# Sums of Strassen products in the GLU units: from VectorE additions to TensorE accumulation seeded by ScalarE

## The chip, the core and the metric

The kernel runs as one launch on one NeuronCore of a Trainium2 chip. Its time is the device time of the launch in microseconds (us), taken as the median of several runs. The engines named here are TensorE (PE in the profile; PEld is its weight load), VectorE (DVE), ScalarE (ACT), GpSimd (POOL) and SyncE (SP), which issues most DMAs. Each engine works through its own instructions in order; between engines there are only semaphores. TensorE writes its products into PSUM, eight banks of 128 x 512 fp32 each.

## The reference

With S = 2048 rows, D = 512 columns and F = 1792 hidden columns:

```python
xn = layernorm(x)
a, b = xn @ Wd_re.T, xn @ Wd_im.T          # 512 x 512
y  = Ws_re @ a - Ws_im @ b                 # 2048 x 2048
h  = gelu(xn @ w_gate) * (xn @ w_up)       # 512 x 1792, tanh form
out = x + y + h @ w_down                   # 1792 x 512
```

## The kernel before

The kernel has three stages. The first makes the layer norm and the sequence transform (names `z`, `m`, `pan`), the second the hidden transform (`y`). The third, from about 399 us to the end, computes the gated part, and the change lies there. All matrix products are done in three passes: each operand is split into a high part (a rounded copy, made by ScalarE, `split_hi`, L68) and a low part (the difference, made by VectorE, `split_lo`, L73), and `mm3` (L81) issues high x high, high x low and low x high.

The third stage runs 28 units, `unit(n)` (L552). A unit computes a block of 256 hidden columns x 1024 rows of gate (n even) or up (n odd) as one step of Strassen's scheme in Winograd's form: seven half-size products instead of eight, each a group of six matmuls over 512 columns (`product`, L462), and their sums. The products are numbered 0 to 6 by the operands they take (`xT0` to `xT6` in the trace). The four blocks of the result are, with p0 to p6 for the products: block (0,0) = p0 + p1; a sum p0 + p5 on which block (0,1) builds by adding p4 and p2 in turn; a sum p0 + p5 + p6 to which p4 is added for block (1,1); and p0 + p5 + p6 + p3 for block (1,0). In the kernel before, p0 stands in bank `a` and is copied by ScalarE to an SBUF tile `p1` (L589); p5, p6 and p3 accumulate one after another in bank `b`, p4 and then p2 in bank `c`; VectorE adds `p1` to bank `b` three times (L590 into `q6`, L600 into `w`, L610 into `p1`), and bank `c` twice (L601 into `w`, L616 into `q6`).

Between the products stand fills: `fill()` (L577) takes from a list the next piece of other TensorE work of the same length, six matmuls of the down projection (`dn`) or, in the first units, of the hidden transform (`y`). `FILL` (L519) gives units 0 and 1 two fills, units 2 to 5 three and all others four. A unit asks for a fill after its third product, after product 1, and twice after product 2; where fewer are allowed the last ones fall out, so that behind product 2 of units 0 and 1 the next unit's product 0 follows at once, and behind that of units 2 to 5 after one fill.

The finished blocks go through `first` and `second`. In even units `first` is `gate` (L468): ScalarE takes the GELU of the block into `s`. In odd units it is `up_1` (L472): VectorE multiplies the block into `s`, ScalarE makes the high part `hh`; `second` is `up_2`, VectorE's low part `hl`. The second halves of the last two blocks are carried into the next unit. `run(share)` places background work between these steps: the splits of the next unit's weights (`wh`, `w` on ScalarE, `wl`, `w` on VectorE; two conversions are begun ahead), of the down weights (`wdh`, `wdl`, in even units and unit 1), sums of weights (`ws`, L424) and, in units 7 to 13, splits of the second half of the rows (`xT`). The order of each engine's instructions is that in which the code issues them; nothing reorders them.

Of the kernel before, what the change touches and what calls it, by code (L numbers as in the profile page):

```python
# [11 lines left out]
AF = mybir.ActivationFunctionType  # L12
# [22 lines left out]
def fnet_geglu_kernel(ctx: ExitStack, tc: tile.TileContext, x, xt, cs, dh, wgu, wd, out):  # L35
# [7 lines left out]
    nc = tc.nc  # L43
# [8 lines left out]
    def slot(name, dtype=F32, shape=(P, D)):  # L52
        return mem.tile(list(shape), dtype, name=name, tag="mem")

    def ps_tile(name):
        return psum.tile([P, D], F32, name=name, tag="ps")
# [24 lines left out]
    def mm3(ps, a, sl, b, first, last, resumed=False, part=slice(3)):  # L81

        for r, (u, v) in list(enumerate(((0, 0), (0, 1), (1, 0))))[part]:
            nc.tensor.matmul(ps, a[u][:, sl], b[v], start=first and r == 0, stop=last and r == 2,  # L84
                             skip_group_check=resumed)

    def cols(j):
        return slice(j * P, (j + 1) * P)
# [206 lines left out]
    def flush():  # L295
        while pend:
            split_lo(*pend.pop(0))
# [63 lines left out]
    def load_xT(sp, t):  # L361
        for d in range(ND):
            load_xr(sp, t, d, xnt[sp, t, d])
# [47 lines left out]
    def load_w(n):  # L411
        if n < 2 * NP:
            wx[n] = [slot("wx", F32, (P, 2, HD)) for _ in range(2)]
            for i in range(2):
                nc.sync.dma_start(wx[n][i].rearrange("p a b -> p (a b)"), wgu[n % NP, i])
# [31 lines left out]
    def split_w(n):  # L447
        for k in range(4):
            split(*weight_split(n, k))

    def load_wd(n):

        for i in range(2 if n < 2 * NP else 0):
            wdl[n // 2, i] = slot("wd")
            nc.sync.dma_start(wdl[n // 2, i], wd[n % NP // 2, i])
# [6 lines left out]
    def product(n, k, ps, first=False):  # L462
        for i in range(2):
            mm3(ps, wl[n, k], cols(i), xT[n // NP, k, i], first and i == 0, i == 1, resumed=not first)
# [17 lines left out]
    def load_acc(n):  # L482
        acc[n] = slot(f"acc{n}")
        nc.sync.dma_start(acc[n], parked[n])
# [25 lines left out]
    carry = []  # L510

    def more_items(q):

        i = q % (NP // 2)
        if i % 2 == 0:
            qs = [q - 1, q] if i else [q]
            items.extend([lambda j=j, p=p: down(qs, j, p) for j in range(SPT) for p in qs])
# [3 lines left out]
    def background(n):  # L521

        work = []

        def splits(f, *args, cost=2):
            t = []

            def begin():
                t.append(f(*args))
                split_hi(*t[0])  # L530
            work.append((begin, lambda: split_lo(*t[0]), cost))

        if 0 < n < 2 * NP - 1:
            for k in range(4):
                splits(weight_split, n + 1, k, cost=2 if k < 3 else 1)
        if n == 1 or n % 2 == 0 and n:
            for i in range(2):
                splits(down_split, n, i)
        if n + 2 < 2 * NP:
            for f in weight_sums(n + 2):  # L540
                work.append((None, f, 1))
        if -7 <= n - NP < 0:
            for i in range(2):
                splits(xT_split, 1, (0, 1, 2, 4, 5, 6, 3)[n - NP + 7], i)
        u = n - NP + 10
        if u in (3, 4):
            work.append((None, lambda: sums_xT(1, u - 3), 6))
        if u == 7:
            work.append((None, lambda: t4_xT(1), 4))
        return work  # L550

    def unit(n):  # L552
        left = FILL.get(n, 4)
        load_w(n + 2)
        if n - NP + 10 in (0, 2):
            load_xT(1, (n - NP + 10) // 2)
        work = background(n)
        total, done, begun = sum(w[2] for w in work), 0, 0

        def run(share):  # L560

            nonlocal done, begun
            upto = share * total
            while work and done + work[0][2] / 2 <= upto:
                begin, end, cost = work.pop(0)
                if begun:
                    begun -= 1
                elif begin:
                    begin()
                end()  # L570
                done += cost
            while begun < min(2, len(work)):
                if work[begun][0]:
                    work[begun][0]()
                begun += 1

        def fill():  # L577
            nonlocal left
            left -= 1
            return items.pop(0)() if items and left >= 0 else lambda: None  # L580

        first, second = (gate, lambda *a: None) if n % 2 == 0 else (up_1, up_2)
        if n % 2 == 0 and n:
            more_items(n // 2 - 1)
        a, b, c = ps_tile("a"), ps_tile("b"), ps_tile("c")
        product(n, 0, a, True)
        product(n, 5, b, True)
        p1, q6, w = slot("p1"), slot("q6"), slot("w")
        nc.scalar.activation(p1, a, AF.Copy)  # L589
        nc.vector.tensor_add(q6, b, p1)  # L590
        while carry:
            carry.pop(0)()
        flush()
        product(n, 4, c, True)
        d0 = fill()
        run(.2)
        d0()
        product(n, 6, b)
        run(.35)
        nc.vector.tensor_add(w, b, p1)  # L600
        nc.vector.tensor_add(w, c, w)  # L601
        product(n, 1, a)
        d1 = fill()
        first(n, (0, 0), a)
        first(n, (1, 1), w)
        second(n, (0, 0), a)
        d1()
        run(.55)
        product(n, 3, b)
        nc.vector.tensor_add(p1, b, p1)  # L610
        second(n, (1, 1), w)
        if n == 0:
            split_w(1)
        run(.75)
        product(n, 2, c)
        nc.vector.tensor_add(q6, c, q6)  # L616
        if n % 2 == 1:
            load_wd(n + 1)
        if n % NP == 1:
            for j in range(SPT):  # L620
                load_acc(n // NP * SPT + j)
        first(n, (1, 0), p1)
        first(n, (0, 1), q6)
        d2, d3 = fill(), fill()
        d2()
        run(1)
        carry.extend([lambda: second(n, (1, 0), p1), lambda: second(n, (0, 1), q6), d3])

    def turn_step(k):

# [143 lines left out]
    for n in range(2 * NP):  # L774
        unit(n)
# [36 lines left out]
```

## Time and profile before

| | |
|---|---|
| time, median of 3 runs | 835.08 us (835.06 to 836.07) |
| time of the profiled execution | 835.21 us |
| its span, first to last instruction | 833.4 us |
| TensorE busy | 828.0 us (99%), 3638 matmuls |
| VectorE busy | 679.6 us (82%) |
| ScalarE busy | 364.8 us (44%) |
| granted TensorE clock, mean | 0.999 of 2.4 GHz |

Busy shares are averages over the three stages. Matmuls overlap: one takes 0.39 us, the next starts 0.227 us after it. The start of a matmul, not its end, tells whether TensorE waited. On ScalarE and VectorE, too, a next instruction may start some 0.1 us before the recorded end of the one ahead.

### The profile page before, as it was taken

What the parts mean: (1) busy time and instruction counts of PE and PEld (TensorE: products, weight loads), DVE (VectorE), ACT (ScalarE), POOL (GpSimd) and SP (SyncE); (2) the same over time, 40 slices, a digit from 0 to 9 for tenths busy, and PEclk for the clock granted to TensorE, in tenths of its full rate; (3) what the DMA queues carried; (4) which work ended last, traced back from release to release, by engine and by line L of the source; (5) the groups of instructions that cost most, each with busy time, mean ns of one, the idle gap of its engine ahead of it and who ended that gap; (6) DMA issues with size and microseconds to landing.
All of it is one profiled execution on the core that took longest, in us unless ns stands there. A gap on an engine that the chain in (4) does not pass through costs nothing.

```text
span 833.4 us, 10707 instructions
## 1 busy us (share of the span) xinstructions
PE 828.0 (99%) x3638; PEld 681.6 (82%) x3638; DVE 679.6 (82%) x1227; ACT 364.8 (44%) x672; POOL 9.5 (1%) x22
## 2 busy tenths in 40 slices
PE   9999999999999999999999999999999999999998
PEld 6888888888888888888888888888888888888886
DVE  6677998979799988999688879889877887776852
ACT  6787544633354335554343344434434334333410
POOL 0000000000100010000000000000000000000000
PEclk9999999999999999999999999999999999999999
DMA  9900448563896929852505310101216322120002
GB/s 335 358 14 1 164 161 282 173 219 115 284 334 224 293 107 324 244 169 67 205 23 177 101 52 30 72 26 51 76 51 215 112 56 73 34 68 25 2 9 93
DMA packets 60711, 112.92 MB, mean 135 GB/s; under 512 B 6864, under 2 KB 6896, under 8 KB 60656
## 3 DMA queue, kind: packets, MB, share of 16 engines
q1 hardware_dynamic: 59376, 108.05, 38.6%
q0 software_dynamic: 1280, 4.20, 1.3%
q8 instruction: 28, 0.46, 0.2%
q14 instruction: 27, 0.22, 0.1%
HBM read 99.61 MB, written 12.60 MB: 135 GB/s over the span
## 4 chain that ended last, share of the span: by engine, by line
PE 94%; DVE 3%; DMA 1%; issue 0%; ACT 0%; DVEq 0%; ACTq 0%
PE m L84 24%; PE dn L84 18%; PE b L84 14%; PE z L84 10%; PE c L84 9%; PE a L84 9%; PE y L84 9%; DVE psl L73 1%; DMA xr<-in_xt 1%; PE warm L658 1%; DVE m L314 1%; DMA wd<-in_wd 0%; DMA pan<-in_cs 0%; DVE ws L424 0%; DVE pan L267 0%
## 5 line engine op out<-in xcount | busy, mean ns | idle before, releaser
L68 ACT ACTIVATE psh<-pan 128x512 fp32r<-128x512 f32 x168 | 97.6, 627 | 106.4 <-DVE pan L267 32.5
L73 DVE TENSOR_TENSOR psl<-pan,psh 128x512 fp32r<-128x512 f32 x168 | 105.3, 684 | 3.8 <-ACT psh L68 3.6
L68 ACT ACTIVATE hh<-s 128x512 fp32r<-128x512 f32 x56 | 34.4, 633 | 125.9 <-DVE s L475 120.8
L84 PE MATMUL dn<-wdh,hh 128*128 128x512 f32 x224 | 87.1, 389 | 0.0
L84 PE MATMUL dn<-wdl,hh 128*128 128x512 f32 x224 | 87.1, 389 | 0.0
L84 PE MATMUL dn<-wdh,hl 128*128 128x512 f32 x224 | 87.1, 389 | 0.0
L84 PE MATMUL m<-psh,xch 128*128 128x512 f32 x192 | 74.8, 389 | 0.0
L84 PE MATMUL m<-psh,xcl 128*128 128x512 f32 x192 | 74.7, 389 | 0.0
L84 PE MATMUL m<-psl,xch 128*128 128x512 f32 x192 | 74.7, 389 | 0.0
L498 DVE TENSOR_TENSOR acc<-dn,acc 128x512 f32<-128x512 f32 x64 | 43.9, 686 | 29.6 <-PE dn L84 29.6
L590 DVE TENSOR_TENSOR q<-b,p 128x512 f32<-128x512 f32 x28 | 19.3, 690 | 43.8 <-PE b L84 42.9
L84 PEld LDWEIGHTS dn<-wdh,hh 128*128 128x128 f32 x224 | 42.0, 188 | 8.8
L84 PEld LDWEIGHTS dn<-wdh,hl 128*128 128x128 f32 x224 | 42.0, 188 | 8.7
L84 PEld LDWEIGHTS dn<-wdl,hh 128*128 128x128 f32 x224 | 42.0, 188 | 8.7
L84 PE MATMUL z<-panh,xa 128*128 128x512 f32 x128 | 44.8, 390 | 0.0
L84 PE MATMUL z<-panh,xb 128*128 128x512 f32 x128 | 44.6, 389 | 0.0
L84 PEld LDWEIGHTS m<-psh,xch 128*128 128x128 f32 x192 | 36.0, 188 | 7.6
L84 PEld LDWEIGHTS m<-psh,xcl 128*128 128x128 f32 x192 | 36.0, 188 | 7.5
L84 PEld LDWEIGHTS m<-psl,xch 128*128 128x128 f32 x192 | 36.0, 188 | 7.4
L73 DVE TENSOR_TENSOR hl<-s,hh 128x512 fp32r<-128x512 f32 x56 | 37.2, 685 | 2.0 <-ACT hh L68 1.4
L73 DVE TENSOR_TENSOR wl<-ws,wh 128x512 fp32r<-128x512 f32 x56 | 36.9, 684 | 0.0
L84 PE MATMUL m<-psh,xc 128*128 128x512 f32 x96 | 33.5, 390 | 0.3 <-DVE yx L228 0.3
(345 smaller groups left out, 1997.7 us busy)
## 6 DMA issues: line engine op xcount, KB each, us to landing
pan<-in_cs SPq DMA_DIRECT2D x200, 256.0 KB, 4.4
wx<-in_wgu SPq DMA_DIRECT2D x56, 256.0 KB, 2.9
wd<-in_wd SPq DMA_DIRECT2D x28, 256.0 KB, 2.8
x<-in_x SPq DMA_DIRECT2D x16, 256.0 KB, 5.4
yx<-in_x SPq DMA_DIRECT2D x16, 256.0 KB, 4.4
parked<-yx SPq DMA_DIRECT2D x16, 256.0 KB, 2.2
xr<-in_xt SPq DMA_DIRECT2D x16, 256.0 KB, 5.5
xnt<-xr POOLq DMA_DIRECT2D x16, 256.0 KB, 3.1
```

The costliest lines, as they stand in the source:

```text
L68: nc.scalar.activation(t[0], src, AF.Copy, scale=float(sign))
L73: engine.tensor_sub(t[1], src, hi)
L84: nc.tensor.matmul(ps, a[u][:, sl], b[v], start=first and r == 0, stop=last and r == 2, skip_group_check=resumed)
L314: nc.vector.tensor_tensor(msb[dst, d], mps[r, d], msb[dst, d], op=op)
L498: nc.vector.tensor_add(acc[n], dps[n], acc[n])
L590: nc.vector.tensor_add(q6, b, p1)
L658: nc.tensor.matmul(ps, warm[:, :P], warm, start=i == 0, stop=i == WARM - 1)
```

## The change

In each unit the SBUF tile `p1` goes. ScalarE copies bank `a` (product 0) into bank `b`, and products 5, 6 and 3 then accumulate on that copy: product 5 is issued without the flag that starts a new sum. Product 4, which was issued third, is issued second, so that bank `b` is first needed one product later; product 5 comes third. The three additions of `p1` on VectorE (L590, L600, L610) go. In place of the first two ScalarE copies bank `b` into `q6` and into `w` (L594 and L600 of the new code); in place of the third the last block is read straight from bank `b` by `first`. VectorE keeps the two additions of bank `c`.

```diff
@@ -584,20 +584,20 @@
             more_items(n // 2 - 1)
         a, b, c = ps_tile("a"), ps_tile("b"), ps_tile("c")
         product(n, 0, a, True)
-        product(n, 5, b, True)
-        p1, q6, w = slot("p1"), slot("q6"), slot("w")
-        nc.scalar.activation(p1, a, AF.Copy)
-        nc.vector.tensor_add(q6, b, p1)
+        q6, w = slot("q6"), slot("w")
+        nc.scalar.activation(b, a, AF.Copy)
+        product(n, 4, c, True)
         while carry:
             carry.pop(0)()
         flush()
-        product(n, 4, c, True)
+        product(n, 5, b)
+        nc.scalar.activation(q6, b, AF.Copy)
         d0 = fill()
         run(.2)
         d0()
         product(n, 6, b)
         run(.35)
-        nc.vector.tensor_add(w, b, p1)
+        nc.scalar.activation(w, b, AF.Copy)
         nc.vector.tensor_add(w, c, w)
         product(n, 1, a)
         d1 = fill()
@@ -607,7 +607,6 @@
         d1()
         run(.55)
         product(n, 3, b)
-        nc.vector.tensor_add(p1, b, p1)
         second(n, (1, 1), w)
         if n == 0:
             split_w(1)
@@ -619,12 +618,12 @@
         if n % NP == 1:
             for j in range(SPT):
                 load_acc(n // NP * SPT + j)
-        first(n, (1, 0), p1)
+        first(n, (1, 0), b)
         first(n, (0, 1), q6)
         d2, d3 = fill(), fill()
         d2()
         run(1)
-        carry.extend([lambda: second(n, (1, 0), p1), lambda: second(n, (0, 1), q6), d3])
+        carry.extend([lambda: second(n, (1, 0), b), lambda: second(n, (0, 1), q6), d3])
 
     def turn_step(k):
```

Three places show the order in which the instructions stand now. On TensorE, at the start of unit 1 (`a` is product 0, `c` product 4, `b` product 5):

```order
 L84 MATMUL a<-xT01l,wh 128x512
 L84 MATMUL a<-xT01h,wl 128x512
+L84 MATMUL c<-xT40h,wh 128x512
+L84 MATMUL c<-xT40l,wh 128x512
+L84 MATMUL c<-xT40h,wl 128x512
+L84 MATMUL c<-xT41h,wh 128x512
+L84 MATMUL c<-xT41l,wh 128x512
+L84 MATMUL c<-xT41h,wl 128x512
 L84 MATMUL b<-xT50h,wh 128x512
 L84 MATMUL b<-xT50l,wh 128x512
```

The same six matmuls of product 4 stood behind the six of product 5 before; all else on TensorE keeps its place. On ScalarE, from the last GELU of unit 0 (`s<-q`) to the first copy of unit 2, before:

```order
L470 ACTIVATE s<-q_4176 128x512
L589 ACTIVATE p_4276<-a 128x512
L68 ACTIVATE wh<-wx 128x512
L68 ACTIVATE wh<-ws 128x512 x2
L68 ACTIVATE w<-wx 128x256
L68 ACTIVATE wdh<-wd 128x512
L68 ACTIVATE hh<-s 128x512 x2
L68 ACTIVATE wdh<-wd 128x512
L68 ACTIVATE hh<-s 128x512 x2
L589 ACTIVATE p_4413<-a 128x512
```

and with the change:

```order
L470 ACTIVATE s<-q_4169 128x512
L588 ACTIVATE b<-a 128x512
L594 ACTIVATE q_4268<-b 128x512
L68 ACTIVATE wh<-wx 128x512
L68 ACTIVATE wh<-ws 128x512 x2
L68 ACTIVATE w<-wx 128x256
L68 ACTIVATE wdh<-wd 128x512
L600 ACTIVATE w<-b 128x512
L68 ACTIVATE hh<-s 128x512 x2
L68 ACTIVATE wdh<-wd 128x512
L68 ACTIVATE hh<-s 128x512 x2
L588 ACTIVATE b<-a 128x512
```

Two copies out of bank `b` have come in, one ahead of the weight conversions and one behind them; the copy of product 0 stands where it stood, behind the last two `hh` of the unit before. On VectorE, the end of unit 1 from the addition that completes `w`, before:

```order
L601 TENSOR_TENSOR w<-c,w 128x512
L475 TENSOR_TENSOR s<-s,a 128x512
L475 TENSOR_TENSOR s<-s,w 128x512
L73 TENSOR_TENSOR hl<-s,hh 128x512
L73 TENSOR_TENSOR w<-wx,w 128x256
L73 TENSOR_TENSOR wdl<-wd,wdh 128x512
L610 TENSOR_TENSOR p_4276<-b,p_4276 128x512
L73 TENSOR_TENSOR hl<-s,hh 128x512
L73 TENSOR_TENSOR wdl<-wd,wdh 128x512
L616 TENSOR_TENSOR q_4277<-c,q_4277 128x512
L475 TENSOR_TENSOR s<-s,p_4276 128x512
L475 TENSOR_TENSOR s<-s,q_4277 128x512
```

and with the change:

```order
L601 TENSOR_TENSOR w<-c,w 128x512
L475 TENSOR_TENSOR s<-s,a 128x512
L475 TENSOR_TENSOR s<-s,w 128x512
L73 TENSOR_TENSOR hl<-s,hh 128x512
L73 TENSOR_TENSOR w<-wx,w 128x256
L73 TENSOR_TENSOR wdl<-wd,wdh 128x512
L73 TENSOR_TENSOR hl<-s,hh 128x512
L73 TENSOR_TENSOR wdl<-wd,wdh 128x512
L615 TENSOR_TENSOR q_4268<-c,q_4268 128x512
L475 TENSOR_TENSOR s<-s,b 128x512
L475 TENSOR_TENSOR s<-s,q_4268 128x512
```

Here one addition is gone and nothing else has moved; the block (1,0) is now read from bank `b` itself.

## Rows read from the trace of the kernel before

**Rows 1.** The page: the span, and busy us (share) xinstructions of each engine

```profile
span 833.4 us, 10707 instructions
...
PE 828.0 (99%) x3638; PEld 681.6 (82%) x3638; DVE 679.6 (82%) x1227; ACT 364.8 (44%) x672; POOL 9.5 (1%) x22
```

**Rows 2.** Busy us (x instructions) in two stretches: PE, PEld, DVE, ACT, POOL; clock, DMA

```profile
360.00:380.00 20.00, 20.00 (x90) 16.53 (x89) 19.73 (x32) 10.28 (x20) 0.00 (x0) 1.00 0.51 162
800.00:820.00 20.00, 20.00 (x90) 16.57 (x89) 11.46 (x18) 2.41 (x4) 0.00 (x0) 1.00 0.10 40
```

**Rows 3.** Groups by line: busy us, mean ns | idle before, what ended it

```profile
L590 DVE TENSOR_TENSOR q<-b,p 128x512 f32<-128x512 f32 x28 | 19.3, 690 | 43.8 <-PE b L84 42.9 <-ACT p L589 0.9
...
L589 ACT ACTIVATE p<-a 128x512 f32<-128x512 f32 x28 | 16.7, 595 | 34.6 <-PE a L84 34.5
```

**Rows 4.** Waits: who waited for whom, us in total, times, longest us

```profile
ACT p L589 <- PE a L84: 34.5, 20, 4.9
```

**Rows 5.** Timeline of PE, start of unit 1: start us, duration, line, operation

```profile
411.65 0.39 PE L84 MATMUL a<-xT00h,wh 128*128 128x512 f32 x1
...
412.78 0.39 PE L84 MATMUL a<-xT01h,wl 128*128 128x512 f32 x1
413.01 0.39 PE L84 MATMUL b<-xT50h,wh 128*128 128x512 f32 x1
...
414.37 0.39 PE L84 MATMUL c<-xT40h,wh 128*128 128x512 f32 x1
```

**Rows 6.** Timeline, places where a matmul stood close behind the VectorE result it needs

```profile
387.55 0.68 DVE L75 SCALAR_TENSOR_TENSOR z100l<-m,z100h 128x512 fp32r<-128x512 f32 x1
...
388.59 0.39 PE L84 MATMUL y<-d4h,z100l 128*128 128x512 f32 x1
...
517.13 0.68 DVE L600 TENSOR_TENSOR w<-b,p 128x512 f32<-128x512 f32 x1
...
517.50 0.39 PE L84 MATMUL dn<-wdh,hl 128*128 128x512 f32 x1
...
517.87 0.50 PE L84 MATMUL b<-xT30h,w 128*128 128x512 f32 x1
518.21 0.39 PE L84 MATMUL b<-xT30l,w 128*128 128x512 f32 x1
```

**Rows 7.** Timeline of ACT, end of unit 0 and the copy of unit 1

```profile
410.12 0.62 ACT L68 ACTIVATE wh<-wx 128x512 fp32r<-128x512 f32 x1
...
414.29 0.63 ACT L470 ACTIVATE s<-q 128x512 f32<-128x512 f32 x1 [1.68 <-DVE q L616]
414.82 0.58 ACT L589 ACTIVATE p<-a 128x512 f32<-128x512 f32 x1
```

**Rows 8.** Timeline of DVE, end of unit 0

```profile
410.49 0.69 DVE L610 TENSOR_TENSOR p<-b,p 128x512 f32<-128x512 f32 x1 [2.33 <-PE b L84]
411.09 0.68 DVE L73 TENSOR_TENSOR wl<-wx,wh 128x512 fp32r<-128x512 f32 x1
...
413.57 0.69 DVE L616 TENSOR_TENSOR q<-c,q 128x512 f32<-128x512 f32 x1
```

**Rows 9.** Timeline of PE, first matmul of product 4 in units 2 and 4

```profile
426.61 0.39 PE L84 MATMUL c<-xT40h,wh 128*128 128x512 f32 x1
...
453.81 0.39 PE L84 MATMUL c<-xT40h,wh 128*128 128x512 f32 x1
```

**Rows 10.** Timeline of ACT, the copies of units 2 and 4

```profile
427.26 0.58 ACT L589 ACTIVATE p<-a 128x512 f32<-128x512 f32 x1
...
453.48 0.58 ACT L589 ACTIVATE p<-a 128x512 f32<-128x512 f32 x1
```

**Rows 11.** Timeline of DVE, end of unit 1

```profile
420.00 0.69 DVE L475 TENSOR_TENSOR s<-s,a 128x512 f32<-128x512 f32 x1
...
423.00 0.68 DVE L610 TENSOR_TENSOR p<-b,p 128x512 f32<-128x512 f32 x1
423.60 0.68 DVE L73 TENSOR_TENSOR hl<-s,hh 128x512 fp32r<-128x512 f32 x1
```

## The prediction

> **What bounds the kernel now.** I read the page's busy shares first: TensorE is busy 99% of the span, VectorE 82% [rows 1]. As matmuls overlap, that 99% alone proves little, so the second view was the busy time in stretches. There 90 matmuls start in 20 us while VectorE is busy 19.73 us of it, and 90 start in 20 us while it is busy 11.46 us [rows 2]. So TensorE's step, 0.2267 us in the timeline ((414.37 - 413.01) / 6, [rows 5]), does not depend on how loaded VectorE is, and only a matmul that starts later than one step after the one ahead is lost time. Third, I followed the starts of the 28 units in the timeline of PE: a unit of seven products and f fills lasts (7 + f) x 1.36 us everywhere, but for unit 8, which is 0.3 us longer. There VectorE's L600 ends at 517.81, and the first matmul of product 3, due at 517.73, starts at 517.87, takes 0.50 and has its next 0.34 behind it [rows 6]. That is the whole loss of the third stage that a lighter VectorE can give back. The rest of the span above TensorE's busy time lies at the start and behind the last matmul, which the change does not touch.
>
> **How a late operand is paid for.** The same rows give the price. The operand came 0.08 us after the matmul was due, and the matmul behind it started at 518.21 instead of 517.95: 0.26 lost. So a result must be there some 0.17 us before the due start, and each later tenth costs a tenth. On the other side, z100l ended 388.23 and its matmul started on its step at 388.59, at a margin of 0.36 without loss [rows 6]. The limit lies in between; I take 0.17. These are VectorE's hand-overs; no row shows a matmul held up by ScalarE, and I use the same limit.
>
> **What is removed and added.** Off VectorE go 3 x 28 additions of 0.69, 58 us by busy time (one of the three groups stands in the rows); on ScalarE come 2 x 28 copies of about 0.60, 33 us, as it does 28 such copies already [rows 3]. Neither engine sets the end, so both sums count as nothing by themselves. The cover is TensorE's own work; the question is where it now has to wait. The number of matmuls is unchanged, and so is their step: in before, too, products accumulate on a bank that another product had begun.
>
> **The new waits.** (1) Product 5 waits for the copy of bank `a` into bank `b`. Before, nothing on TensorE waited for that copy. The product ends at 413.17, 1.52 us after its first matmul started, and product 5 is due 2.72 us after it, where product 4's first matmul stands today (414.37, [rows 5]). An unhindered copy starts 0.03 later (that is what passes from the end of q's addition at 414.26 to the GELU at 414.29, [rows 7, 8]) and takes 0.60: it ends at 2.15, a margin of 0.57, above the 0.36 seen to cost nothing. The duration of a copy that writes PSUM is in no row. I bound it below by 0.29, half of the 0.58 of today's copy, and above by the 0.69 that VectorE needs for a bank; I take 0.58 to 0.60, from today's copy, which reads the same bank. The ends change the two stalls below by -0.3 or +0.1 each, and neither opens a stall in the other units.
> The Trainium skill ("ScalarE: Activation LUTs", section "Step-by-step: what each stage is for") calls PSUM the lower-latency destination for ScalarE. No run here shows it so far; by an estimate that grants the 0.03 between the 0.595 of a bank's copy and the 0.62 of a conversion from SBUF once more, the sum below would be 0.06 smaller.
> (2) Product 6 waits for the copy of `b` into `q6`. Before, VectorE's L590 had a product and a fill to read `b`; now it is the fill alone. Product 5 ends 1.52 after its start, the copy ends 0.63 later, product 6 is due at 2.72: margin 0.57 again. ScalarE is free, as it has just waited for product 5. (3) Product 3 waits for the copy into `w`; ScalarE has at most six conversions between the two copies, 5 x 0.52 + 0.31, begun 0.6 us after product 5 ends, and the product is due 5.3 us after that end: covered. (4) Bank `b` is held until `first` has read it; its next user comes a product or more later in every unit, so nothing.
> What queues behind the waiting copy on ScalarE: the weight conversions start about 2.8 us later in a unit, and VectorE's low parts with them. They are needed by the next unit, and VectorE has three additions less to do.
>
> **Where the copy is late.** In 20 of 28 units ScalarE stands idle before its copy, waiting for product 0 [rows 4]. In others it comes late, since the copy stands behind the last GELU or the last `hh` of the unit before, which wait for VectorE.
> - Unit 1. The copy ended at 415.40 [rows 7], where the new limit is 414.37 - 0.17 = 414.20: with nothing gained, 1.20 us. It stood behind the GELU of `q6`, that behind L616 at 413.57, that behind low parts that followed L610 [rows 8]. L610 goes, but the first low part can't come up from 411.09 by a whole 0.60: its high part ends at 410.74 [rows 7], so it starts at 410.78, 0.31 earlier. The copy then ends at 415.09: 0.9 us lost.
> - Unit 2. The copy ended at 427.84 [rows 10], the limit is 426.61 - 0.17 = 426.44 [rows 9]: 1.40 with nothing gained. The chain before it starts with `s<-s,a` at 420.00, which waited for product 1, so it moves with TensorE; in it L610 occupied VectorE from 423.00 to 423.60 [rows 11], and 0.60 is gained. The new copy into `w` stands behind five conversions and may give up to 0.1 back. 1.40 - 0.60 + 0.1 = 0.9 us lost.
> - Units 4, 6, 8 and 12. Four copies came 0.8 to 0.9 us after their product; unit 4's ended at 454.06 with a limit of 453.64 [rows 9, 10], 0.42 over, the others within 0.06 of that. The same L610 stands in each chain, and 0.60 less puts each under the limit by 0.1 to 0.2: nothing, but not by much.
> - Unit 8's old stall goes: its copy into `w` is ScalarE's and ends long before product 3. -0.26.
>
> Sum: 0.9 + 0.9 - 0.26 = +1.5 us. Against the profiled execution's own 835.21 (span 833.4 and 1.8 around it) that is 836.7; that execution lies 0.13 above the median of 835.08, so 836.6 as a median, 0.18% more.
>
> **Rivals.**
> A, slower: VectorE does not get ahead. Its low parts now start only when the copy into `q6` and a conversion are done, some 1.3 us later than today, and if this eats the 0.60 gained by L610 wherever the copy was late, all six stalls are paid in full: 1.20 + 1.40 + 0.42 and about 0.4 to 0.5 for each of three more, 4.3 in all, less 0.26: 839.1. It decides from the point at which `s<-s,a` no longer waits for product 1. For it: VectorE is full to 19.73 of 20 us in a stretch [rows 2]. Against: 43.8 us of idle time stood before L590 in the kernel before [rows 3], so the later start falls into a time that was idle.
> B, slower: the margin of 0.57 is not enough in all units, because a write into PSUM or its hand-over to TensorE takes longer. It decides from 0.4 us more than I count; beyond that each 0.1 us costs 28 x 2 x 0.1 = 5.6 us, since two such waits stand in each unit, 840 and more. Against: VectorE's hand-over at 0.36 cost nothing [rows 6].
> C, no change: the two early stalls are covered, as the GELU of unit 0 or the chain in unit 1 comes up by more than I allow; if the copy of unit 1 gained the whole 0.60 and unit 2's chain 0.3 more, +0.6 + 0.6 - 0.26 = +0.9, and with the short copy of 0.29 +0.3: 835.4 to 836.0.
> D, faster: less traffic of VectorE quickens the matmuls. A step shorter by 1% over the 400 us of the third stage would save 4 us: 831. [Rows 2] speak against it.
>
> **How the numbers follow.** What a measurement of this kernel can tell from no change is about 0.2%, 1.67 us. The forecast of about 1.0 to 2.3 us more has 0.55; it lies across that bound, and I put 0.33 of it within and 0.22 above. A has 0.15, B 0.07, both slower; C 0.18, within; D and whatever else is faster 0.05. Together: faster 0.05, within 0.51, slower 0.44. The range runs from 834.9, below C, to 838.9, just under A's full price; B, D and the ends of A are left out, some 0.15.
>
> **What would show it.** In the new profile L590, L600 and L610 of before are gone from VectorE, which falls by about 58 us, and ScalarE rises by about 33. TensorE shows gaps of about 0.9 us before the first `b<-xT50h` of units 1 and 2, waiting for ScalarE, and none in the other units; unit 8 lasts 14.96. Gaps before `b<-xT50h` in units 4, 6, 8 and 12 would mean A, small ones in every unit B, none at all C, and a step other than 0.2267 D. I am wrong in the mechanism if TensorE waits for VectorE or for a transfer anywhere that it did not before.

## The result and the profile after

| | before | changed |
|---|---|---|
| median time | 835.37 us (13 runs) | 837.08 us (13 runs) |
| ratio, with 95% interval | | 1.0018 (1.0011 to 1.0026) |
| profiled execution, its span | 835.21, 833.4 us | 837.27, 835.5 us |

The change makes the kernel 1.7 us longer, 0.9 to 2.2 by the interval; forecast were 1.5. The page of the changed kernel, in the columns of [rows 1]:

```profile
span 835.5 us, 10637 instructions
...
PE 828.0 (99%) x3638; PEld 681.0 (82%) x3638; DVE 629.2 (75%) x1143; ACT 394.6 (47%) x728; POOL 9.5 (1%) x22
```

TensorE has the same work. VectorE is 50 us less busy (84 instructions fewer), ScalarE 30 us more (56 more); 58 and 33 were forecast from the durations, but instructions that follow each other overlap by some 0.1 us, so that an addition less frees 0.60 rather than 0.69, and a copy more takes 0.53 rather than 0.60. The same two stretches as in [rows 2], for the changed kernel:

```profile
360.00:380.00 20.00, 20.00 (x90) 16.57 (x89) 19.76 (x32) 10.41 (x20) 0.00 (x0) 1.00 0.47 161
800.00:820.00 20.00, 20.00 (x90) 16.57 (x89) 9.71 (x15) 3.07 (x5) 0.00 (x0) 1.00 0.09 34
```

Again 90 matmuls in both: the lighter VectorE has not moved TensorE's step. The groups that answer to [rows 3], the copies first:

```profile
L594 ACT ACTIVATE q<-b 128x512 f32<-128x512 f32 x28 | 16.7, 598 | 59.1 <-PE b L84 59.1
L600 ACT ACTIVATE w<-b 128x512 f32<-128x512 f32 x28 | 16.5, 591 | 7.4 <-PE b L84 7.4
L588 ACT ACTIVATE b<-a 128x512 f32<-128x512 f32 x28 | 16.3, 582 | 41.6 <-PE a L84 41.6
L84 PE MATMUL b<-xT50h,wh 128*128 128x512 f32 x28 | 11.1, 397 | 1.2 <-ACT b L588 1.2
```

The last row has no counterpart before: TensorE is idle 1.2 us before product 5, waiting for the copy into bank `b`. What TensorE waits for, in total, times and longest:

```profile
PE warm L657 <- DVE eps L654: 1.2, 1, 1.2
PE b L84 <- ACT b L588: 1.2, 2, 0.6
PE z L84 <- ACT xa L122: 0.8, 1, 0.8
PE m L84 <- DVE yx L228: 0.3, 1, 0.3
PE y L84 <- DVE z110l L75: 0.2, 1, 0.2
```

The wait for the copy occurs twice. (Idle time counts from the end of the matmul ahead, which overlaps; the loss is read from the starts.) TensorE at the start of unit 1, as in [rows 5]:

```profile
412.23 0.39 PE L84 MATMUL a<-xT00h,wh 128*128 128x512 f32 x1
...
414.73 0.39 PE L84 MATMUL c<-xT41h,wl 128*128 128x512 f32 x1
415.73 0.50 PE L84 MATMUL b<-xT50h,wh 128*128 128x512 f32 x1 [0.62 <-ACT b L588]
416.07 0.40 PE L84 MATMUL b<-xT50l,wh 128*128 128x512 f32 x1
```

From 414.73 to 416.07 two steps have passed in 1.34 us instead of 0.45. ScalarE at that place, as in [rows 7]:

```profile
414.56 0.63 ACT L470 ACTIVATE s<-q 128x512 f32<-128x512 f32 x1 [1.40 <-DVE q L615]
415.10 0.58 ACT L588 ACTIVATE b<-a 128x512 f32<-128x512 f32 x1
```

Product 0 was complete at 413.75, 1.52 after its start; the copy starts only at 415.10, behind the GELU of unit 0's last block, which waited for VectorE. The copy ends at 415.68 and product 5 starts 0.05 later. The chain that ends there passes in unit 0 through an instruction that stands only once in the third stage, the load of ScalarE's function table ahead of the first GELU:

```profile
408.39 1.28 ACT L470 ACT_TABLE_LOAD   x1 [0.81 <-PE a L84]
```

It waits for product 1 of unit 0 and takes 1.28 us; the GELUs, the high parts of the next weights and VectorE's low parts follow it. The same wait in unit 2, TensorE, and ScalarE's copy there:

```profile
427.88 0.39 PE L84 MATMUL c<-xT41h,wl 128*128 128x512 f32 x1
428.81 0.50 PE L84 MATMUL b<-xT50h,wh 128*128 128x512 f32 x1 [0.54 <-ACT b L588]
429.15 0.39 PE L84 MATMUL b<-xT50l,wh 128*128 128x512 f32 x1
```

```profile
428.17 0.58 ACT L588 ACTIVATE b<-a 128x512 f32<-128x512 f32 x1
```

The lengths of the units, from the first matmul of one to that of the next, in excess of (7 + fills) x 1.36 us:

| | unit 1 | unit 2 | unit 8 | others | unit 0 to unit 27 |
|---|---|---|---|---|---|
| before | 0 | 0 | 0.29 | 0 | 393.32 |
| changed | 0.91 | 0.84 | 0 | 0 | 394.80 |

So the third stage lasts 1.48 us longer. The remaining 0.57 of the two spans' difference lies ahead of unit 0, which begins at 399.41 before and at 399.98 after the change, where TensorE waited 0.8 for the first `xa`. In the six kernels below, whose first two stages are the same, unit 0 begins anywhere from 399.43 to 399.77, so that part varies with no change in those stages; how much of it belongs to the change can't be told from one profile of each kernel.

### The profile page after: what moved, and what is told of

Its sections match the earlier page's. It is cut to its first block, busy times and chain, and to the rows that moved or that the text cites. A ratio compares the mean times of both kernels' runs of the same rounds, so it can differ in the third digit from the quotient of the medians.

```text
span 835.5 us, 10637 instructions
## 1 busy us (share of the span) xinstructions
PE 828.0 (99%) x3638; PEld 681.0 (82%) x3638; DVE 629.2 (75%) x1143; ACT 394.6 (47%) x728; POOL 9.5 (1%) x22
## 4 chain that ended last, share of the span: by engine, by line
PE 92%; DVE 4%; DMA 2%; ACT 1%; issue 1%; DVEq 0%; ACTq 0%; SPq 0%
PE m L84 24%; PE dn L84 18%; PE b L84 13%; PE z L84 10%; PE y L84 9%; PE a L84 9%; PE c L84 8%; DVE psl L73 1%; DMA xr<-in_xt 1%; DVE m L314 1%; DMA wd<-in_wd 1%; DMA x<-in_x 0%; DMA pan<-in_cs 0%; ACT wh L68 0%; DVE wl L73 0%
## 5 line engine op out<-in xcount | busy, mean ns | idle before, releaser
L73 DVE TENSOR_TENSOR wl<-wx,wh 128x512 fp32r<-128x512 f32 x28 | 19.4, 692 | 82.4 <-ACT wh L68 82.4
L594 ACT ACTIVATE q<-b 128x512 f32<-128x512 f32 x28 | 16.7, 598 | 59.1 <-PE b L84 59.1
```

Source lines behind the costliest of these rows:

```text
L73: engine.tensor_sub(t[1], src, hi)
L594: nc.scalar.activation(q6, b, AF.Copy)
```

## The experiments

**Units 1 and 2 as before.** Is the loss all in two units? These two go back to the old scheme; the other branches on `old` are of the same kind:

```diff
+        old = n in (1, 2)
+        if old:
+            product(n, 5, b, True)
+            p1, q6, w = slot("p1"), slot("q6"), slot("w")
+            nc.scalar.activation(p1, a, AF.Copy)
+            nc.vector.tensor_add(q6, b, p1)
+        else:
...
```

> Units 1 and 2 alone go back to the scheme of before (product 0 into an SBUF tile, three additions on VectorE, product 5 second); the other 26 units keep the seeded banks. Theory (all of the loss is two late copies, in units 1 and 2, 0.9 us each): both gaps go, unit 8 keeps its 0.3 us gain, so 0.3 us less than before, about 835.1 at a before of 835.4 (ratio 0.9996). Rival 1 (part of the loss, the 0.57 us by which unit 0 began later, belongs to the change): 0.3 us above before. Rival 2 (a small cost in every unit): near the changed kernel, 837, at least 1 us above before.

Measured: 835.36 us, ratio to before 1.0000 (0.9991 to 1.0009). In its profile no matmul of the third stage waits; unit 0 to unit 27 take 393.07 us, 0.25 less than before, unit 8's gap being gone. Rival 2 falls. For the third stage the length bears out the theory. Rival 1 speaks of the time ahead of unit 0, which that length leaves open: the interval of the time, 0.75 us to either side, holds its +0.3 as well as the theory's -0.3, and unit 0 begins at 399.77 here.

**Another spread of the fills.** If the copy is only late, a place behind a fill must cure it:

```diff
-    FILL = {0: 2, 1: 2, 2: 3, 3: 3, 4: 3, 5: 3}
+    FILL = {0: 3, 1: 3, 2: 2, 3: 3, 4: 2, 5: 3}
```

> The changed kernel with another spread of the fills: units 0, 1, 3 and 5 three each, units 2 and 4 two each (before: 2, 2, 3, 3, 3, 3), so that one piece of other work stands between product 2 of units 0 and 1 and the next product 0. Theory: each copy has 1.36 us more until product 5 needs it; the gaps of 0.92 and 0.83 go and units 3 and 5 open none, as ScalarE stood idle 1.36 us before their copies: 835.1, a ratio to before of 0.9996. Rival (the copy needs more than a place behind a fill, or the two units robbed of one begin to wait): 836 or more, with gaps at product 5 of units 3 or 5.

Measured: 835.33 us, ratio 0.9998 (0.9989 to 1.0007); unit 0 to unit 27 take 393.05 us, with no unit off its length. ScalarE at the start of unit 1 of this kernel, and TensorE's product 0 and product 5 there:

```profile
414.22 0.63 ACT L470 ACTIVATE s<-q 128x512 f32<-128x512 f32 x1 [1.40 <-DVE q L615]
414.81 0.58 ACT L588 ACTIVATE b<-a 128x512 f32<-128x512 f32 x1
```

```profile
413.25 0.39 PE L84 MATMUL a<-xT00h,wh 128*128 128x512 f32 x1
...
415.97 0.39 PE L84 MATMUL b<-xT50h,wh 128*128 128x512 f32 x1
```

The GELU is as late as ever, but product 0 comes 1.36 us later; the copy ends at 415.39, 0.58 ahead of product 5. With the seeded banks kept in all units the loss is gone, and the kernel is level with before: on TensorE there is nothing that the freed VectorE could give back but unit 8's gap, 0.27 us by the stage's length.

**One addition back on VectorE.** The prediction rested the copies of units 4, 6, 8 and 12 on the 0.60 us that L610 no longer takes:

```diff
         product(n, 3, b)
+        extra = slot("extra")
+        nc.vector.tensor_add(extra, w, w)
```

> The changed kernel with one VectorE addition per unit put back at the place of the removed L610, on SBUF tiles and with a result nobody reads. Theory (that addition's 0.60 us is what keeps the copies of units 4, 6, 8 and 12 in time): unit 2 loses 0.6 us more, units 4 and 6 open gaps of 0.3, units 8 and 12 of 0.4 to 0.5, unit 1 is unchanged as VectorE is idle ahead of it: 2.2 us more than the changed kernel, 839.3, ratio to before 1.0047. Rival (VectorE's load has no part in it): as the changed kernel, 837.1, no new gap.

The added instruction does not wait for product 3, as L610 did; it puts back VectorE's load alone. Measured: 839.45 us, ratio 1.0047 (1.0035 to 1.0060), 2.4 above the changed kernel (2.7 by the length of the stage). The excess of the units: 0.91 in unit 1, 1.47 in unit 2, 0.41 and 0.42 in units 4 and 6, 0.70 and 0.50 in units 8 and 12, nothing elsewhere. Unit 2 lost 0.63 more, unit 1 nothing more, the four others opened. Unit 8 of this kernel, TensorE and ScalarE:

```profile
514.18 0.39 PE L84 MATMUL c<-xT41h,wl 128*128 128x512 f32 x1
514.98 0.50 PE L84 MATMUL b<-xT50h,wh 128*128 128x512 f32 x1 [0.41 <-ACT b L588]
```

```profile
512.92 0.63 ACT L68 ACTIVATE hh<-s 128x512 fp32r<-128x512 f32 x1 [4.84 <-DVE s L475]
513.80 0.63 ACT L68 ACTIVATE hh<-s 128x512 fp32r<-128x512 f32 x1 [0.25 <-ACT hh L68]
514.34 0.58 ACT L588 ACTIVATE b<-a 128x512 f32<-128x512 f32 x1
```

The chain stands there link by link: VectorE's product into `s`, ScalarE's `hh`, the copy behind it, TensorE. Taking this one addition per unit off VectorE is worth 2.4 us here, though VectorE is not the bound: it keeps ScalarE in time.

**The copy done twice.** The price of a late seed, measured in every unit:

```diff
         nc.scalar.activation(b, a, AF.Copy)
+        nc.scalar.activation(b, a, AF.Copy)
```

> The changed kernel with the copy of bank a into bank b done twice, the second waiting for the first. Each seed is then ready about 0.62 us later, 0.03 us after product 5 is due. Theory (a matmul is held up from 0.17 us before its due time on): 0.2 us lost in each of 22 units that lose nothing now, 0.3 to 0.5 in units 4, 6, 8 and 12, 0.6 more in units 1 and 2: 6 to 7.3 us above the changed kernel, 843 to 844.4. If ScalarE's hand-over needs no such lead, 3.2 us: 840.3. If the limit lies at 0.36, 10 us or more: 847.

Measured: 843.98 us, ratio 1.0102 (1.0088 to 1.0115), 6.9 above the changed kernel. Unit 7 of it, ScalarE and TensorE:

```profile
498.45 0.58 ACT L588 ACTIVATE b<-a 128x512 f32<-128x512 f32 x1 [2.72 <-PE a L84]
499.06 0.58 ACT L589 ACTIVATE b<-a 128x512 f32<-128x512 f32 x1
```

```profile
499.38 0.39 PE L84 MATMUL c<-xT41h,wl 128*128 128x512 f32 x1
499.70 0.50 PE L84 MATMUL b<-xT50h,wh 128*128 128x512 f32 x1
500.03 0.39 PE L84 MATMUL b<-xT50l,wh 128*128 128x512 f32 x1
```

The seed is ready at 499.64, 0.03 after product 5's due start of 499.61, and the second matmul is 0.20 late. Each ordinary unit loses 0.22, 21 of them by their lengths. So ScalarE's hand-over to TensorE has the price of VectorE's [rows 6]: lateness plus 0.17 by the start of the second matmul, plus about 0.2 by the length of the unit. Units 4, 6, 8 and 12 lose 0.34 to 0.49 and unit 2 1.40, 0.56 more than in the changed kernel, as expected. Unit 1 is a miss inside the sum that came out: it loses 0.74, less than the 0.91 of the changed kernel, where 0.6 more was expected. Its chain began earlier:

```profile
407.40 1.28 ACT L470 ACT_TABLE_LOAD   x1
```

Here the load of the function table did not wait for product 1 of unit 0. It began 4.62 us ahead of unit 1, in the changed kernel 3.84 ahead, and 0.78 earlier less 0.61 for the second copy is the 0.17 that unit 1 lost less. So unit 1's loss hangs on where this one load stands; why it stood ahead of the wait in this kernel alone is open.

**Seeded banks without the move.** Product 5 in second place, as before:

```diff
-        product(n, 4, c, True)
+        product(n, 5, b)
+        nc.scalar.activation(q6, b, AF.Copy)
         while carry:
             carry.pop(0)()
         flush()
-        product(n, 5, b)
-        nc.scalar.activation(q6, b, AF.Copy)
+        product(n, 4, c, True)
```

> The changed kernel with product 5 left in second place and product 4 in third, as before: the seeded banks alone, without the move. Theory (a matmul is held up from 0.17 us before its due time; the unhindered copy ends 2.15 us after product 0 begins, and product 5 is due at 1.36): 0.96 us lost in each of 28 units, 26.9 in all, and up to 3 us more where the copy comes late as well (units 1, 2, 4, 6, 8, 12): 862.5 to 865.3 at a before of 835.4. Rival (TensorE has other work queued that it can take in the meantime, or the wait is only for part of the bank): a few us.

Measured: 866.79 us, ratio 1.0373 (1.0356 to 1.0390), 1.5 above the expected range; the one of its four runs at a granted clock of 1.000 took 865.82, 0.5 above it, so the fall of the clock told below need not be the whole of the miss. Of the 27 units whose length can be read, 21 lose 0.96 or 0.97, as reckoned; units 4, 6, 8 and 12 lose 1.07 to 1.26, unit 1 2.27, unit 2 3.81. TensorE's waits in this kernel:

```profile
PE b L84 <- ACT b L588: 22.1, 28, 2.0
```

Unit 2 is what the expectation missed, and not by the wait. TensorE there, and busy us by engine in the stretch that follows it (PE, PEld, DVE, ACT, POOL; granted clock, DMA share, GB/s):

```profile
430.54 0.50 PE L84 MATMUL b<-xT50h,wh 128*128 128x512 f32 x1 [1.88 <-ACT b L588]
...
431.86 0.63 PE L84 MATMUL b<-xT51h,wl 128*128 128x512 f32 x1
432.29 0.63 PE L84 MATMUL c<-xT40h,wh 128*128 128x512 f32 x1
```

```profile
431.60:435.00 3.40, 3.40 (x10) 2.62 (x9) 1.74 (x4) 2.47 (x6) 0.00 (x0) 0.52 0.02 5
```

From 431.86 to 434.85 the matmuls start 0.43 us apart: the granted clock stood at its lower level, after two waits of about 1.9 us, one in unit 1 and one here. Of unit 2's 3.81 us the gap itself is 2.15 (428.28 to 430.88, less two steps); of the other 1.66, 1.6 is lost in this stretch, by the starts.

**The move without seeded banks.** The kernel before, with products 4 and 5 exchanged:

```diff
-        product(n, 5, b, True)
         p1, q6, w = slot("p1"), slot("q6"), slot("w")
         nc.scalar.activation(p1, a, AF.Copy)
-        nc.vector.tensor_add(q6, b, p1)
+        product(n, 4, c, True)
         while carry:
             carry.pop(0)()
         flush()
-        product(n, 4, c, True)
+        product(n, 5, b, True)
+        nc.vector.tensor_add(q6, b, p1)
```

> The kernel before with product 4 in second and product 5 in third place, and nothing else: three additions on VectorE, no seeded bank. Theory: no wait is new on ScalarE, and VectorE's first addition has the fill alone as cover, which suffices as ScalarE's copy does in the changed kernel: no gap at product 6, unit 8 keeps its 0.3, as before, 835.4 (ratio 1.000). Rival (the order itself, not the late copies, costs the 1.7 us): 837.

Measured: 837.36 us, ratio 1.0020 (1.0011 to 1.0030): the expectation was wrong, and the rival's number came out. But the place is another than in the changed kernel:

```profile
PE b L84 <- DVE q L594: 1.2, 2, 0.7
```

TensorE waits for VectorE, before product 6: units 2, 6, 8 and 12 last 0.81, 0.18, 1.01 and 0.21 too long, unit 4 0.03, unit 1 nothing. Unit 8's loss, too, lies all before product 6; its old gap at product 3 does not show. VectorE in unit 2 of this kernel:

```profile
428.06 0.42 DVE L424 TENSOR_TENSOR ws<-wx,ws 128x256 f32<-128x256 f32 x1
428.40 1.28 DVE L73 TENSOR_TENSOR hl<-s,hh 128x512 fp32r<-128x512 f32 x2
429.60 0.68 DVE L594 TENSOR_TENSOR q<-b,p 128x512 f32<-128x512 f32 x1
```

and TensorE:

```profile
429.43 0.39 PE L84 MATMUL y<-d7h,z111l 128*128 128x512 f32 x1
430.34 0.50 PE L84 MATMUL b<-xT60h,wh 128*128 128x512 f32 x1 [0.52 <-DVE q L594]
430.68 0.40 PE L84 MATMUL b<-xT60l,wh 128*128 128x512 f32 x1
```

The first addition of the unit stands on VectorE behind the two low parts carried over from unit 1, without a gap, and ends 0.6 after product 6 is due. I had given it the cover that ScalarE's copy has in the changed kernel, and overlooked that VectorE is not free at that time: in this edit the carried parts come first. With the addition ahead of them, as before, it might fare better or delay those parts; that wasn't tried. So the seed needs the move, by the experiment before this one, and in this order of VectorE's instructions the move in turn needs `q6` to be read by an engine that is free when product 5 ends.

## Why the prediction was right

The mechanism held, and the third stage came out 1.48 us longer where the sum had 1.5. The medians differ by 1.71; the 0.2 more lies within the interval, and no run assigns it.

- *What bounds.* TensorE's step is the same in all eight kernels wherever the clock was full, and 84 additions off VectorE brought back nothing but unit 8's gap: 0.29 against the 0.26 in the sum.
- *The unhindered copy.* Most of the changed kernel's 28 copies end 0.58 to 0.59 before product 5, forecast 0.57, and those into `q6` leave 0.5 to 0.57 as forecast, but for unit 0's, which left 0.23 and cost 0.01. ScalarE's copy into PSUM took 0.582 against 0.598 and 0.591 for reads of a bank into SBUF (L588, L594 and L600 above). This agrees in sign with the lower latency that the Trainium skill ("ScalarE: Activation LUTs", section "Step-by-step: what each stage is for") states. It is 0.01 to 0.02 us, too little to matter in the sum.
- *Unit 1.* 0.9 forecast, 0.91 measured. The forecast took the start of the high part over from the kernel before as it stood there, and did not ask what holds it: it stands behind the load of the function table, which waited for product 1 in both kernels and so moved with TensorE. Had the load stood as in the kernel with two copies, 0.78 earlier, about 0.1 would have been left of the 0.91 (an estimate from these two kernels; no run shows it). The bound by the high part shows in VectorE's row of the changed kernel, where the low part now waits for ScalarE instead of following L610 [rows 8]:

```profile
411.36 0.69 DVE L73 TENSOR_TENSOR wl<-wx,wh 128x512 fp32r<-128x512 f32 x1 [2.71 <-ACT wh L68]
```

- *Unit 2.* 0.9 forecast, 0.84 measured; the 0.1 that I added for the copy into `w` was a little too much.
- *Units 4, 6, 8 and 12.* None lost anything: their copies end 0.30 to 0.46 ahead of product 5, against the limit of 0.17. Putting one addition back opened all four. So the 0.60 was gained, and nothing ate it, as rival A had supposed; without that gain the four stalls stand where A has them. In unit 8 that kernel paid 0.70, where rival A has 0.4 to 0.5.
- *The limit of 0.17* was read from one VectorE hand-over and carried over to ScalarE without a row to show it. That it held, with 0.22 in each ordinary unit of the kernel with two copies against 0.03 + 0.17, the prediction could not know.
- *Rivals.* B and D fall by the unit lengths, C by the two gaps. The forecast size, 0.18%, is the measured one, and the ratio's interval, 0.11% to 0.26%, lies only a little clear of no change.
- *The sign of being wrong*, a new wait of TensorE for VectorE, did not come. The 0.2 us for `z110l` among the waits above lies ahead of unit 0, and before the change TensorE waited there as well, 0.5 us at its weight load.
- *What it lacked* is the move of product 4 as a cause of its own. The text asked whether ScalarE is free to copy `b` into `q6`, and so found the cover; it did not see that leaving the addition on VectorE, behind the carried parts, would have cost as much as the whole change.

## What to carry to other kernels

Where one engine is the bound and keeps its step, taking work off another is worth only the gaps that it ends; list those first (here one of 0.3 us) and then ask for each new wait what stands ahead of the instruction waited for, in its own engine's queue. An instruction that comes only once, as the load of the function table here, can stand there too. A result that only an SBUF tile needed becomes a condition for the bounding engine once it is the seed of its accumulation: it then needs a place with slack in every unit, in the shortest ones too, and either a fill behind the last product or a producer without late work ahead of it gives that. Work taken off an engine that is not the bound can still be what keeps the next in time: the additions taken off VectorE were worth 0.3 us before the change, and one of the three in each unit 2.4 us after it.

## What the runs showed of the hardware

In these kernels a matmul whose operand came late cost the lateness and some 0.2 us on top, whether VectorE handed it over (0.81 for 0.62 late, product 6 of unit 2 in the kernel with the move alone) or ScalarE (0.22 for 0.03 late, with two copies). With the operand 0.23 us ahead of the due start 0.01 was lost, with 0.21 ahead 0.03 (product 6 of unit 0, changed kernel and one addition back), with 0.30 nothing. And two waits of about 1.9 us on TensorE, in units 1 and 2 of the kernel with product 5 in second place, were followed by one fall of the granted clock to its lower level (0.52 in a stretch of 3.4 us, 0.43 us a matmul), 1.6 us in all; after the shorter waits of the changed kernel it stood at 1.00. ScalarE's load of its function table took 1.28 us, once in the third stage, and in one of eight kernels it ran ahead of a wait that held it in the other seven.
